# Layer two's attention for the even tokens on VectorE, beside layer one's second GEMM for the odd tokens

## The chip, the cores and the metric

The kernel runs on one core of one Trainium2 chip. The metric is the device time of one execution in microseconds (us); lower is better. A profiled execution gives the trace that the text reads. PE is TensorE, DVE is VectorE, ACT is ScalarE, SP is the engine whose queue issues every DMA of this kernel.

## The reference

Two layers of the same form, on 2048 tokens of width 1024, in bf16. Each layer first adds an attention of 32 heads of width 32, in which a token looks at itself and at the seven tokens 2, 4, ..., 14 places before it, and then adds a token-mixing MLP of hidden width 3584. Both read a layer norm without gains.

```python
W, dil = 8, 2
idx = pos[:, None] - (jnp.arange(W) * dil)[None, :]
logits = einsum("bhsd,bhswd->bhsw", q, kg) * scale     # kg, vg: k and v gathered at idx
logits = where(idx >= 0, logits, -1e9)
o = einsum("bhsw,bhswd->bhsd", softmax(logits), vg)    # then @ wo
u = gelu(einsum("bsd,sf->bdf", layernorm(x), w1) + b1)
y = einsum("bdf,fs->bds", u, w2) + b2
# x = x + attention(layernorm(x)); x = x + y(layernorm(x)); both twice, same weights
```

Since the step is 2, even tokens look at even tokens alone and odd ones at odd ones. The MLP mixes all tokens.

## The kernel before

Tokens are kept by class: `c` is 0 for even and 1 for odd tokens, `i` counts the eight tiles of 128 tokens in a class (`SC` = 1024 tokens). `hT` holds the normalised activations, features on partitions, the columns in class order. Each of the two layers runs four stages in this order, all bound together by PE's program order:

1. The V projection, 16 tiles of 128 tokens (`v_proj`, line 337; in the first layer `V_`, line 255).
2. Attention, in 16 units of one head group `g` (four heads) and one class `c`. A unit has two visits `b`. A visit computes `scores` (line 383), ACT's exponential (line 386), the band `mask` on DVE (line 398), `values` (lines 414 to 431), and two of the four `qk_chunk` (line 352) of the next unit. A chunk's queries go to `qB`, four copies for four heads: two on DVE (line 363), two by SP's DMAs (line 365).
3. The output projection `out_proj` (line 467) with the residual and the layer norm. The first four of its 16 tiles lie in the last two visits.
4. `gemm1` (line 510) with gelu, and `gemm2` (line 553): for each `i` the weights `w2` are loaded once, and both classes are computed. A `gemm2` step (c, i) is 56 matmuls of 128x512; DVE then adds bias and residual (line 556, twice), and in the first layer takes the statistics (lines 180 and 182), ACT makes the factor (lines 174 and 175), DVE normalises (line 188), and SP issues the store of `xb` and the transposing DMA to `hT` (line 562).

The order on an engine is set when the program is built: a scheduler places the instructions, `chain_` and `tc.issue_after` force an order among those that they name, and at run time every engine and every queue works in its order. Buffers come from pools with a fixed number: the PSUM tiles `m` (2), `s` (2) and `acc` (1), the weights' pool `wp` (9 tiles, tag `w`), `x2p` (6). A new tile waits until the tile whose place it takes is free. `qB`, `kT` and `Pm` have fixed places of their own before the change.

Of the kernel before, what the change touches and what calls it, by code (L numbers as in the profile page):

```python
# [17 lines left out]
W = 8  # L18
# [7 lines left out]
def kernel(  # L26
# [52 lines left out]
    pcp = pool("pcp", 2)  # L79
    dram = pool("dram", 1, space=bass.MemoryType.DRAM)  # L80
# [66 lines left out]

    hT = pers.tile([P, KD, S], BF16, name="hT")
    qB = [pers.tile([P, HG, SC + W], BF16, name=f"qB{n}") for n in range(2)]
    kT = [pers.tile([P, SC], BF16, name=f"kT{n}") for n in range(2)]  # L150
    Pm = pers.tile([P, HG, NS * HB, KW], BF16, name="Pm")

    def zero_fill():
        nc.vector.memset(Pm[:].rearrange("p h t k -> p (h t k)"), 0.0)
        for t in qB:
            r = nc.vector.memset(t[:].rearrange("p h t -> p (h t)"), 0.0)
        return r
# [8 lines left out]
    w1_v = B_w1.rearrange("(i p c) f -> c p i f", p=P, c=DIL)  # L166
    w2_v = B_w2.rearrange("(ft p) s -> p ft s", p=P)

    def rows(t, c, i):
        return t[(c * NI + i) * P:(c * NI + i + 1) * P, :]  # L170

# [156 lines left out]
    def fill_wv(wv, n):  # L328
        for hf in range(2):
            nc.sync.dma_start(out=wv[n][hf][:],  # L330
                              in_=wq_v[:, hf * (KD // 2):(hf + 1) * (KD // 2), 2 * D + n * 512:2 * D + (n + 1) * 512])

# [14 lines left out]
    def qk_chunk(u, wts, part, n):  # L347
        g, c = divmod(u, DIL)
# [44 lines left out]
    def mask(*rs):  # L393
        pc, s0 = exps
        for r in rs:
# [6 lines left out]
    def values(u, b, v, oT):  # L402
        g, c = divmod(u, DIL)
        acc = a_tile()
        t0 = b * HB
# [52 lines left out]
    def out_proj(c, i, oT, wo, res, dst, h2):  # L458
# [17 lines left out]
        def store():  # L476
            nc.sync.dma_start(out=rows(dst, c, i), in_=xn[:])
            h2[c][i] = vhp.tile([P, D], BF16, name="h2", tag="vh")
# [10 lines left out]
    def load_w1(fb):  # L489
        tiles = []  # L490
        for c in range(DIL):
            t = wt_("w1", [P, NI, FB])
            r = nc.sync.dma_start(out=t[:], in_=w1_v[c, :, :, fb * FB:(fb + 1) * FB])
# [6 lines left out]
    def gemm1(fb, h2, g):  # L500
        if fb not in w1s:
            load_w1(fb)
# [61 lines left out]
    NU = NG * DIL  # L564
    for li in range(2):
        first = li == 0
        v = [[None] * NI for _ in range(DIL)]
        for c, i in order:
            v[c][i] = vhp.tile([P, D], BF16, name="v", tag="vh")
# [6 lines left out]
        else:  # L576
            fill_wv(wv, 0)
            fill_wv(wv, 1)
            wts = [None, None]
            chain_("SP", load_qk, 0, wts)  # L580
            for i in range(NI):
                for c in range(DIL):
                    v_proj(v, c, i, wv, (0, 1))
            res = lambda c, i: rows(xb, c, i)
        oT = [gop.tile([P, S], BF16, name="oT", tag="go") for _ in range(NG)]
        h2 = [[None] * NI for _ in range(DIL)]
# [5 lines left out]
        for vis in range(2 * NU):  # L592
            u, b = divmod(vis, 2)
            if b == 0 and u % (2 * DIL) == 1 and u + 3 < NU:
                nxt = [None, None]
                chain_("SP", load_qk, u // (2 * DIL) + 1, nxt)
            if b == 0 and (u + 1) % (2 * DIL) == 0 and u + 1 < NU:
# [19 lines left out]
            for n in range(2):  # L617
# [3 lines left out]
                half, add, store, ln = out_proj(0, 2 * b + n, oT, wo, res, xa[li], h2)  # L621
# [12 lines left out]
        for k, (c, i) in enumerate(order[4:]):  # L634
            if k in (8, 10):
                chain_("SP", load_w1, k // 2 - 4)
            half, add, store, ln = out_proj(c, i, oT, wo, res, xa[li], h2)
# [10 lines left out]
        for fb in range(NFB):  # L648
            gemm1(fb, h2, g)
        if first:  # L650
            ln_exp_table()
        for i in range(NI):
            w2t = load_w2(i)
            w1s.clear()
            for c in range(DIL):
                gemm2(c, i, w2t, g, xa[li], rows(xb, c, i) if first else out_v[c, i], first)


# [28 lines left out]
```

The softmax here doesn't subtract the row's maximum and nothing guards it: scores larger than these inputs give would overflow.

## Time and profile before

| | us |
|---|---|
| median of three runs (lowest, highest) | 1298.24 (1298.19, 1298.45) |
| the profiled execution: its time / its span | 1297.71 / 1296.0 |
| PE busy / DVE busy / ACT busy | 1288.2 / 419.3 / 373.4 |
| first layer's `gemm2`, from its first matmul to the V projection after it | 457.84 to 651.06 |
| second layer's V projection, from its first matmul on | 651.06 to 706.48 |
| second layer's visits with `qk_chunk` (30 of 32) | 713.4 to 846.5 |

The span runs from the first to the last instruction that the profile shows; the time of the same execution is 1.7 us longer. The profiled execution is 0.5 us shorter than the median. Instructions of one engine are in order. A matmul's busy time overlaps that of the next one, since they are pipelined: what a matmul costs is read from the distance of the starts.

### The profile page before, as it was taken

To read this page: it belongs to the slowest core of one execution; us is meant where nothing else is said; L and a number is where in the kernel's file an instruction comes from. 1 tells how busy PE (TensorE), PEld (TensorE's weight loads), DVE (VectorE), ACT (ScalarE), POOL (GpSimd) and SP (SyncE) were. 2 spreads that over 40 slices of the span, in tenths; PEclk is the share of its full clock that TensorE was granted. 3 is DMA by queue.
4 is the path that set the end of the run, shared out by engine and by line. 5 is a ranking of instruction groups with operands and counts; after the bars stand their busy time and mean duration, and the time that the engine had idled before them with its cause. 6 is when DMAs were issued, how large, how long until landed. Compare 5 with 4: busy or idle time off the path is not lost.

```text
span 1296.0 us, 19495 instructions
## 1 busy us (share of the span) xinstructions
PE 1288.2 (99%) x8414; PEld 591.7 (46%) x8414; DVE 419.3 (32%) x851; ACT 373.4 (29%) x628; POOL 2.4 (0%) x15
## 2 busy tenths in 40 slices
PE   9999999999999999999999999999999999999998
PEld 4444444444444444444444444444444444444443
DVE  7457778810000022322300667688000000111111
ACT  5456665531111110000023666654211111000000
POOL 0000000000000000000000000000000000000000
PEclk9999999999999999999999999999999999999999
DMA  8411123652222235465510111246423222334330
GB/s 235 82 45 47 51 82 115 208 145 82 65 82 75 57 108 140 130 160 135 130 32 1 48 49 50 80 150 211 122 65 91 73 60 84 98 106 140 113 92 33
DMA packets 201574, 125.54 MB, mean 97 GB/s; under 512 B 39824, under 2 KB 183184, under 8 KB 201488
## 3 DMA queue, kind: packets, MB, share of 16 engines
q1 hardware_dynamic: 201488, 124.30, 33.8%
q8 instruction: 66, 1.08, 0.4%
q14 instruction: 20, 0.16, 0.0%
HBM read 96.48 MB, written 16.78 MB: 87 GB/s over the span
## 4 chain that ended last, share of the span: by engine, by line
PE 97%; DVE 1%; ACT 1%; issue 0%; DMA 0%; SPq 0%; DVEq 0%
PE m L352 17%; PE s L553 15%; PE s L510 15%; PE m L553 7%; PE m L510 7%; PE acc L510 7%; PE acc L553 7%; PE m L467 7%; PE m L337 4%; PE m L255 4%; PE s L383 2%; PE acc L418 1%; PE acc L422 1%; DVE xn L474 0%; PE m L268 0%; DVE Pm L398 0%
## 5 line engine op out<-in xcount | busy, mean ns | idle before, releaser
L510 PEld LDWEIGHTS <-w 128*128 128x128 bf16 x1792 | 175.4, 98 | 211.4
L553 PEld LDWEIGHTS <-w 128*128 128x128 bf16 x1792 | 175.3, 98 | 211.5
L352 PE MATMUL m<-hT,wqk 128*128 128x512 bf16 x1024 | 231.7, 380 | 0.0
L510 PE MATMUL s<-h,w 128*128 128x512 bf16 x896 | 202.8, 379 | 0.0
L553 PE MATMUL s<-g,w 128*128 128x512 bf16 x896 | 199.9, 379 | 0.0
L556 DVE SCALAR_TENSOR_TENSOR xo<-s,b_sb,xs 128x512 bf16<-128x512 f32 x32 | 24.0, 751 | 540.7 <-PE s L553 538.6
L352 PEld LDWEIGHTS <-wqk 128*128 128x128 bf16 x1024 | 95.3, 98 | 117.9 <-issue 10.7
L398 DVE TENSOR_TENSOR Pm<-pc,band 32x640 bf16<-32x640 bf16 x256 | 123.6, 483 | 65.8 <-ACT pc L386 56.3
L467 PE MATMUL m<-wo,oT 128*128 128x512 bf16 x512 | 112.5, 379 | 1.2 <-DVE xn L474 1.1
L510 PE MATMUL acc<-h,w 128*128 128x512 bf16 x448 | 103.9, 379 | 0.0
L553 PE MATMUL acc<-g,w 128*128 128x512 bf16 x448 | 100.6, 379 | 0.0
L553 PE MATMUL m<-g,w 128*128 128x512 bf16 x448 | 99.3, 379 | 0.0
L510 PE MATMUL m<-h,w 128*128 128x512 bf16 x448 | 99.0, 379 | 0.0
L174 ACT ACTIVATE ln<-mv,eps 128x1 f32<-128x1 f32 x64 | 18.9, 295 | 233.3 <-DVE mv L182 227.6
L517 ACT ACTIVATE g<-s,b_sb 128x1024 bf16<-128x1024 f32 x28 | 31.2, 1114 | 166.9 <-PE s L510 166.9
L467 PEld LDWEIGHTS <-oT 128*128 128x128 bf16 x512 | 49.5, 98 | 62.6 <-issue 4.5
L363 DVE COPY qB<-qs 32x512 bf16<-32x512 bf16 x136 | 38.1, 280 | 90.4 <-ACT qs L359 89.1
L255 PE MATMUL m<-wv,hT 128*128 128x512 bf16 x256 | 56.1, 379 | 0.7 <-ACT hT L249 0.7
L337 PE MATMUL m<-wv,hT 128*128 128x512 bf16 x256 | 55.4, 379 | 0.0
L359 ACT CAST qs<-m 128x512 bf16<-128x512 f32 x64 | 37.5, 586 | 49.0 <-PE m L352 49.0
L386 ACT ACTIVATE pc<-s,shift 128x640 bf16<-128x640 f32 x64 | 51.2, 799 | 0.3 <-PE s L383 0.3
L356 ACT CAST kT<-m 128x512 bf16<-128x512 f32 x64 | 37.5, 586 | 46.4 <-PE m L352 46.4
(57 smaller groups left out, 674.7 us busy)
## 6 DMA issues: line engine op xcount, KB each, us to landing
w<-in_B_w_dram SPq DMA_DIRECT2D x56, 512.0 KB, 3.8
w<-in_B_w_dram SPq DMA_DIRECT2D x64, 448.0 KB, 4.6
wqk<-in_A_wqkv_dram SPq DMA_DIRECT2D x16, 512.0 KB, 4.8
xa<-xn SPq DMA_DIRECT2D x32, 256.0 KB, 2.3
xs<-xa SPq DMA_DIRECT2D x32, 256.0 KB, 3.2
wv<-in_A_wqkv_dram SPq DMA_DIRECT2D x8, 512.0 KB, 5.5
wo<-in_A_wo_dram SPq DMA_DIRECT2D x8, 512.0 KB, 5.5
xr<-in_A_x_dram SPq DMA_DIRECT2D x16, 256.0 KB, 3.3
```

What stands on the lines that cost most here:

```text
L255: r = nc.tensor.matmul(pss_[k, n][:], lhsT=hT[:, kt, cols(*order[k])], rhs=wv[n][kt // 4][:, kt % 4, :], start=(kt == 0), stop=(kt == KD - 1))
L337: nc.tensor.matmul(ps[:], lhsT=hT[:, kt, cols(c, i)], rhs=wv[n][kt // 4][:, kt % 4, :], start=(kt == 0), stop=(kt == KD - 1))
L352: mm = nc.tensor.matmul(ps[:], lhsT=wts[part][:, kt, (g % 2) * P:(g % 2 + 1) * P], rhs=hT[:, kt, lo:lo + 512], start=(kt == 0), stop=(kt = ...
L356: nc.scalar.copy(out=kT[u % 2][:, ls], in_=ps[:])
L359: nc.scalar.copy(out=qs[:], in_=ps[:])
L363: nc.vector.tensor_copy(out=qB[u % 2][hp, h, ls], in_=qs[hp, :])
L386: nc.scalar.activation(out=pc[:].rearrange("p (n t) h k -> p n (t h k)", n=2), in_=ss[:, :, 0:2 * HG * GW], func=ACT.Exp, scale=scale, bia ...
L398: mm = nc.vector.tensor_tensor(out=Pm[rp, :, s0:s0 + HB, r * KG:r * KG + GW].rearrange("p h t k -> p t h k"), in0=pc[rp], in1=mk, op=ALU.mult)
L467: mm = nc.tensor.matmul(ps[:], lhsT=oT[g][:, cols(c, i)], rhs=wo[n][g // 4][:, g % 4, :], start=(g == 0), stop=(g == NG - 1))
L510: nc.tensor.matmul(pairs[fl][0][dc], lhsT=wt[c][:, i, fl * P:(fl + 1) * P], rhs=h2[c][i][:, dc * 512:(dc + 1) * 512], start=(k == 0), stop ...
L517: nc.scalar.activation(out=g[fb][:, fl, :].rearrange("p (n d) -> p n d", n=2), in_=t[:], func=ACT.Gelu_apprx_tanh, bias=b1_sb[:, ft:ft + 1])
L553: nc.tensor.matmul(aps[dc], lhsT=w2t[ft // HF][:, ft % HF, c::DIL], rhs=g[ft // GF][:, ft % GF, dc * 512:(dc + 1) * 512], start=(ft == 0), ...
```

## The change

In the second layer the attention of the even tokens leaves the units on PE, so that 16 units become 8 (the odd class alone). It is done by a class `Early`, which works while the first layer's `gemm2` still has odd tiles to do. The first layer's `gemm2` is reordered: all eight even tiles, the first odd tile, and then steps "C" (projections of one head group of the even tokens) alternate with the other odd tiles "G"; two C steps come first. The weights `w2` are now loaded once for each (c, i).

`Early` puts eight consecutive even tokens in each partition (token 8p + i in partition p, row i). `proj` computes q, k and v of one head group with `hT` columns of step 8 as the stationary operand: for each `i` eight matmuls with 256 moving columns and eight with 128. ACT copies q to `Q`, and k and v to rows 7 to 14 of `KV`, which has two places (`g % 2`). `halo` copies rows 8 to 14 of each partition to rows 0 to 6 of the next one, by one SBUF-to-SBUF DMA of 127 rows of 1792 elements. `qk` multiplies on DVE and adds in a tree, in two halves of four offsets each; `softmax` and `pv` follow one group later. The results go through eight transposing DMAs into `oT`, whose even columns are then in another order; `rows_p` and `w1_p` carry this order on. The tiles of `Early` share the places of `qB`, `kT` and `Pm`, which become pools.

```diff
+    atq = pool("atq", 2)
+    atk = pool("atk", 2)
+    atp = pool("atp", 1)
...
+    early = const.tile([P, W, NI], BF16, name="early")
+    nc.gpsimd.memset(early[:], 1.0)
+    nc.gpsimd.affine_select(out=early[:], in_=early[:], compare_op=ALU.is_ge, fill=0.0, base=1 - W,
+                            pattern=[[1, W], [1, NI]], channel_multiplier=NI)
...
+    def att_tiles():
+        qB[:] = [atq.tile([P, HG, SC + W], BF16, name="qB", tag="qB") for _ in range(2)]
+        kT[:] = [atk.tile([P, SC], BF16, name="kT", tag="kT") for _ in range(2)]
+        Pms[:] = [atp.tile([P, HG, NS * HB, KW], BF16, name="Pm", tag="Pm")]
 
...
+    w1_p = B_w1.rearrange("(p i c) f -> c p i f", i=NI, c=DIL)
+    def rows_p(t, c, i):
+        return t[c * SC:(c + 1) * SC, :].rearrange("(p i) d -> i p d", i=NI)[i]
 
...
+    def gemm2_first(c, i, w2t, k):
+        xs = x2("xs")
+        chain_("SP", lambda: nc.sync.dma_start(out=xs[:], in_=rows(xa[0], c, i)))
+        xo = x2("xo")
+        t = a_tile() if k % 3 == 2 else s_tile()
+
+        def mms():
+            for ft in range(FT):
+                for dc in range(NDC):
+                    r = nc.tensor.matmul(t[:, dc, :], lhsT=w2t[ft // HF][:, ft % HF, c::DIL],
+                                         rhs=g[ft // GF][:, ft % GF, dc * 512:(dc + 1) * 512],
+                                         start=(ft == 0), stop=(ft == FT - 1))
+            return r
+
+        def out():
+            for dc in range(NDC):
+                ds_ = slice(dc * 512, (dc + 1) * 512)
+                nc.vector.scalar_tensor_tensor(out=xo[:, ds_], in0=t[:, dc, :], scalar=b2_sb[:, i, c:c + 1],
+                                               in1=xs[:, ds_], op0=ALU.add, op1=ALU.add)
+            chain_("SP", lambda: nc.sync.dma_start(out=rows(xb, c, i), in_=xo[:]))
+            mean, rs = stats(xo, 1.0, eps1)
+            norm_dve(xs[:], xo[:], mean, rs)
+            chain_("SP", lambda: nc.sync.dma_start_transpose(out=hT[:, :, cols(c, i)], in_=xs[:]))
+
+        return mms, out
+
+    def load_w2c(i, tiles):
+        for n in range(NW2):
+            t = wt_("w2", [P, HF, 256])
+            r = nc.sync.dma_start(out=t[:], in_=w2_v[:, n * HF:(n + 1) * HF, i * 256:(i + 1) * 256])
+            tiles.append(t)
+        return r
+
+    TG = W // 2
+
+    class Early:
+        def __init__(self):
+            self.KV = atp.tile([P, 2, 2 * NI - 1, 2 * P], BF16, name="KV", tag="Pm")
+            nc.vector.memset(self.KV[0:1].rearrange("p b t k -> p (b t k)"), 0.0)
+            self.A = atq.tile([P, TG, NI, P], BF16, name="A", tag="qB")
+            self.Pe = atq.tile([P, TG, NI, P], BF16, name="Pe", tag="qB")
+            self.Q, self.wq, self.wv, self.S, self.EP, self.O = {}, {}, {}, {}, {}, {}
+
+        def load(self, g):
+            self.wq[g] = t = wt_("wqk", [P, KD, 2 * P])
+            for part in range(2):
+                r = nc.sync.dma_start(out=t[:, :, part * P:(part + 1) * P],
+                                      in_=wq_v[:, :, part * D + g * P:part * D + (g + 1) * P])
+            if g % 2 == 0:
+                self.wv[g] = self.wv[g + 1] = t = wt_("wv", [P, KD, 2 * P])
+                r = nc.sync.dma_start(out=t[:], in_=wq_v[:, :, 2 * D + g * P:2 * D + (g + 2) * P])
+            return r
+
+        def proj(self, g):
+            self.Q[g] = atk.tile([P, NI, P], BF16, name="Q", tag="kT")
+            for i in range(NI):
+                ps = m_tile()
+                for kt in range(KD):
+                    nc.tensor.matmul(ps[:, 0:2 * P], lhsT=hT[:, kt, i:SC:NI], rhs=self.wq[g][:, kt, :],
+                                     start=(kt == 0), stop=(kt == KD - 1))
+                for kt in range(KD):
+                    r = nc.tensor.matmul(ps[:, 2 * P:3 * P], lhsT=hT[:, kt, i:SC:NI],
+                                         rhs=self.wv[g][:, kt, (g % 2) * P:(g % 2 + 1) * P],
+                                         start=(kt == 0), stop=(kt == KD - 1))
+                nc.scalar.copy(out=self.Q[g][:, i, :], in_=ps[:, 0:P])
+                nc.scalar.copy(out=self.KV[:, g % 2, NI - 1 + i, :], in_=ps[:, P:3 * P])
+            return r
+
+        def halo(self, g):
+            return nc.sync.dma_start(out=self.KV[1:P, g % 2, 0:W - 1, :], in_=self.KV[0:P - 1, g % 2, NI:NI + W - 1, :])
+
+        def qk(self, g, hf):
+            A = self.A
+            if hf == 0:
+                self.S[g] = pcp.tile([P, W * NI * HG], FP32, name="S", tag="pc")
+            for j in range(TG):
+                s = hf * TG + j
+                nc.vector.tensor_tensor(out=A[:, j], in0=self.Q[g][:], in1=self.KV[:, g % 2, s:s + NI, 0:P], op=ALU.mult)
+            Av = A[:].rearrange("p j i (h d) -> p (j i h) d", d=DH)
+            n = TG * NI * HG
+            w = DH // 2
+            while w > 1:
+                nc.vector.tensor_tensor(out=Av[:, :, 0:w], in0=Av[:, :, 0:w], in1=Av[:, :, w:2 * w], op=ALU.add)
+                w //= 2
+            r = nc.vector.tensor_tensor(out=self.S[g][:, hf * n:(hf + 1) * n], in0=Av[:, :, 0], in1=Av[:, :, 1], op=ALU.add)
+            if hf:
+                self.EP[g] = pcp.tile([P, 2, W * NI * HG], BF16, name="EP", tag="pc")
+                nc.scalar.activation(out=self.EP[g][:, 0, :], in_=self.S[g][:], func=ACT.Exp, scale=scale, bias=shift[:])
+            return r
+
+        def softmax(self, g):
+            E, Pn = self.EP[g][:, 0, :], self.EP[g][:, 1, :]
+            Ev = E.rearrange("p (s h) -> p s h", h=HG)
+            mk = early[:].rearrange("p j i -> p (j i)").unsqueeze(2).to_broadcast([P, W * NI, HG])
+            nc.vector.tensor_tensor(out=Ev, in0=Ev, in1=mk, op=ALU.mult)
+            n = NI * HG
+            dn = x2("den", [P, 7 * n], FP32)
+            ds_ = [dn[:, 0:4 * n], dn[:, 4 * n:6 * n], dn[:, 6 * n:7 * n]]
+            nc.vector.tensor_tensor(out=ds_[0], in0=E[:, 0:4 * n], in1=E[:, 4 * n:8 * n], op=ALU.add)
+            nc.vector.tensor_tensor(out=ds_[1], in0=ds_[0][:, 0:2 * n], in1=ds_[0][:, 2 * n:4 * n], op=ALU.add)
+            nc.vector.tensor_tensor(out=ds_[2], in0=ds_[1][:, 0:n], in1=ds_[1][:, n:2 * n], op=ALU.add)
+            nc.vector.reciprocal(ds_[2], ds_[2])
+            return nc.vector.tensor_tensor(out=Pn.rearrange("p (j n) -> p j n", n=n), in0=E.rearrange("p (j n) -> p j n", n=n),
+                                           in1=ds_[2].unsqueeze(1).to_broadcast([P, W, n]), op=ALU.mult)
+
+        def pv(self, g, hf):
+            Pe = self.Pe
+            if hf == 0:
+                self.O[g] = vhp.tile([P, NI, P], BF16, name="o", tag="vh")
+            n = NI * HG
+            O = self.O[g]
+            for j in range(TG):
+                s = hf * TG + j
+                nc.scalar.copy(out=Pe[:, j].rearrange("p i (h d) -> p (i h) d", d=DH),
+                               in_=self.EP[g][:, 1, s * n:(s + 1) * n].unsqueeze(2).to_broadcast([P, n, DH]))
+                nc.vector.tensor_tensor(out=Pe[:, j], in0=Pe[:, j], in1=self.KV[:, g % 2, s:s + NI, P:2 * P], op=ALU.mult)
+            nc.vector.tensor_tensor(out=Pe[:, 0:2], in0=Pe[:, 0:2], in1=Pe[:, 2:4], op=ALU.add)
+            if hf == 0:
+                return nc.vector.tensor_tensor(out=O[:], in0=Pe[:, 0], in1=Pe[:, 1], op=ALU.add)
+            nc.vector.tensor_tensor(out=Pe[:, 0], in0=Pe[:, 0], in1=Pe[:, 1], op=ALU.add)
+            return nc.vector.tensor_tensor(out=O[:], in0=O[:], in1=Pe[:, 0], op=ALU.add)
+
+        def to_oT(self, g, oT):
+            return nc.sync.dma_start_transpose(out=oT[g][:, 0:SC].rearrange("p (i q) -> p i q", q=P),
+                                               in_=self.O[g][:].rearrange("p i d -> p (i d)"))
+
     for li in range(2):
         first = li == 0
+        units[:] = [(g, c) for g in range(NG) for c in range(DIL) if first or c]
+        NU = len(units)
+        UP = 2 * NU // NG
+        att_tiles()
         v = [[None] * NI for _ in range(DIL)]
         for c, i in order:
-            v[c][i] = vhp.tile([P, D], BF16, name="v", tag="vh")
+            if first or c:
+                v[c][i] = vhp.tile([P, D], BF16, name="v", tag="vh")
         wv = load_wv()
         if first:
             start_up(v, wv)
...
             chain_("SP", load_qk, 0, wts)
             res = lambda c, i: xin_v[c, i]
         else:
-            fill_wv(wv, 0)
-            fill_wv(wv, 1)
+            chain_("SP", fill_wv, wv, 0)
+            chain_("SP", fill_wv, wv, 1)
             wts = [None, None]
             chain_("SP", load_qk, 0, wts)
+            zero_fill()
             for i in range(NI):
-                for c in range(DIL):
-                    v_proj(v, c, i, wv, (0, 1))
-            res = lambda c, i: rows(xb, c, i)
+                v_proj(v, 1, i, wv, (0, 1))
+            res = lambda c, i: (rows if c else rows_p)(xb, c, i)
         oT = [gop.tile([P, S], BF16, name="oT", tag="go") for _ in range(NG)]
+        if not first:
+            for n in range(NG):
+                chain_("SP", ea.to_oT, n, oT)
+        dst = lambda c, i: (rows if c or first else rows_p)(xa[li], c, i)
+        w1_c = [w1_v[c] if first else (w1_v if c else w1_p)[c] for c in range(DIL)]
...
-            gemm1(fb, h2, g)
-        if first:
-            ln_exp_table()
-        for i in range(NI):
-            w2t = load_w2(i)
-            w1s.clear()
-            for c in range(DIL):
-                gemm2(c, i, w2t, g, xa[li], rows(xb, c, i) if first else out_v[c, i], first)
-
-
+            gemm1(fb, h2, g, w1_c)
+        w1s.clear()
+        if not first:
+            for i in range(NI):
+                w2t = load_w2(i)
+                for c in range(DIL):
+                    gemm2(c, i, w2t, g, xa[1], out_v[c, i], False)
+            continue
+        ln_exp_table()
+        ea = Early()
+        steps = [("G", 0, i) for i in range(NI)] + [("G", 1, 0), ("C", 0), ("C", 1)]
+        for i in range(1, NI):
+            steps.append(("G", 1, i))
+            if i + 1 < NI:
+                steps.append(("C", i + 1))
+        wts_ = {}
+
+        def prefetch(k):
+            if k < len(steps):
+                if steps[k][0] == "G":
+                    wts_[k] = []
+                    chain_("SP", load_w2c, steps[k][2], wts_[k])
+                else:
+                    chain_("SP", ea.load, steps[k][1])
+
+        prefetch(0)
+        nk = 0
+        for k, sp_ in enumerate(steps):
+            prefetch(k + 1)
+            if sp_[0] == "G":
+                mms, fin = gemm2_first(sp_[1], sp_[2], wts_[k], nk)
+                nk += 1
+                chain_("PE", mms)
+                fin()
+                continue
+            n = sp_[1]
+            chain_("PE", ea.proj, n)
+            chain_("SP", ea.halo, n)
+            if n:
+                chain_("DVE", ea.softmax, n - 1)
+            chain_("DVE", ea.qk, n, 0)
+            if n:
+                chain_("DVE", ea.pv, n - 1, 0)
+            chain_("DVE", ea.qk, n, 1)
+            if n:
+                chain_("DVE", ea.pv, n - 1, 1)
+        chain_("DVE", ea.softmax, NG - 1)
+        for hf in range(2):
+            chain_("DVE", ea.pv, NG - 1, hf)
```

The built order of one round on the engines, for group n in step C(n), is this. DVE: `softmax`(n-1), `qk`(n) first half, `pv`(n-1) first half, `qk`(n) second half, `pv`(n-1) second half, with the eight DVE instructions of one odd `gemm2` tile strewn in. ACT: the exponential of group n, the `KV` copies of the first two rows of group n+1, then its other `Q` and `KV` copies, with four of the eight broadcast copies to `Pe` of group n between them. SP: `halo`(n), the next projection weights, the next tile's `xs`, `xb` and `hT`, the next `w2`, `halo`(n+1). After the last group ACT has its eight `Pe` copies ahead of the second layer's V copies.

## The prediction

> **What bounds the kernel now.** I read the page's engine shares and chain first, then the busy time by stretches, then the groups of the stages concerned, then the DMA issues.
>
> ```profile
> PE 1288.2 (99%) x8414; PEld 591.7 (46%) x8414; DVE 419.3 (32%) x851; ACT 373.4 (29%) x628; POOL 2.4 (0%) x15
> PE 97%; DVE 1%; ACT 1%; issue 0%; DMA 0%; SPq 0%; DVEq 0%
> 550.00:600.00 50.00, 50.00 (x233) 22.69 (x232) 14.60 (x25) 1.99 (x8) 0.00 (x0) 1.00 0.55 140
> 750.00:800.00 50.00, 49.72 (x648) 24.02 (x647) 35.61 (x81) 33.56 (x57) 0.00 (x0) 1.00 0.22 59
> ```
>
> The first two lines are the page's shares and the chain: PE is the bound everywhere. The other two are stretches (length, then busy time of PE, PEld, DVE, ACT and POOL, the granted clock, DMA share, GB/s). In the first layer's `gemm2` DVE has 35 of 50 us free and ACT 48: that is the room the new attention gets. In the second layer's visits PE is as full.
>
> **PE: removed and added.** Thirty visits with chunks take 713.4 to 846.5, 4.44 us each. Sixteen of them go: 71.0 us. Half of the V projection goes: 55.4/2 = 27.7. Of a visit's 4.44 us, 16 x 0.216 = 3.46 are projections (32 matmuls of 512 columns take 6.91 in the chain), and these come back in `proj`. So the attention that leaves PE is worth 0.98 x 16 = 16 us only. The price of `proj` comes from this:
>
> ```profile
> 9.15 0.62 PE L244 MATMUL s<-ident,x 128*128 128x128 bf16 x8
> 9.61 1.89 PE L255 MATMUL m<-wv,hT 128*128 128x512 bf16 x8
> ```
>
> Eight matmuls of 128 columns, each with its own weight load, take 0.46, so 57 ns each; 256 columns lie between 57 and 216, about 110. One row i is 8 x 110 + 8 x 57 = 1.34 us, a C step 10.7, eight of them 85.6. Net on PE: 71.0 + 27.7 - 85.6 = 13 us less. That is all there is to win.
>
> **DVE per head group.** No row shows a bf16 product of 1024 columns; the nearest are these (group, busy us, mean ns):
>
> ```profile
> L398 DVE TENSOR_TENSOR Pm<-pc,band 32x640 bf16<-32x640 bf16 x256 | 123.6, 483 | 65.8 <-ACT pc L386 56.3
> L474 DVE TENSOR_TENSOR xn<-m,xr 128x512 bf16<-128x512 f32 x64 | 43.8, 685 | 7.4 <-PE m L467 6.1
> L192 DVE TENSOR_SCALAR bi<-mv,rs 128x1 f32<-128x1 f32 x32 | 6.6, 207 | 1.4 <-ACT rs L175 1.2
> ```
>
> From the 640-column row with the 207 ns of a one-column instruction as fixed part, 1024 columns cost 0.65 us and 2048 cost 1.09; in proportion 0.77 and 1.55. I take the middle, 0.71 and 1.30, and 0.03 between neighbours (the four masks of a visit take 2.03 for 4 x 0.483). The dear end is the 512-column row, where one column costs about 1 ns: 1.2 and 2.3. Then a half of `qk` is 4 products, additions over 2048, 1024, 512 and 256 columns and a last one: 2.84 + 1.30 + 0.71 + 0.41 + 0.30 + 0.27 + 0.27 = 6.1. `pv`'s first half is 2.84 + 1.30 + 0.71 + 0.18 = 5.0, the second 5.8, of which 3.0 up to its last product. `softmax` has six small ones: 1.9. The odd tile's own work is 2 x 0.75 + 2 x 0.69 + 0.21 + 0.55, with gaps 3.8. A round of DVE is 6.1 + 5.0 + 6.1 + 5.8 + 1.9 + 3.8 = 28.7 us, against PE's 10.7 + 12.1 (`gemm2`: 193.2/16 a tile) = 22.8. DVE becomes the bound by its work alone.
>
> **The round is also a ring.** `KV` has two places, so the ACT copies of group n+1 wait until DVE's last product of `pv`(n-1) has read its place. They hold the two `m` tiles, so PE stops after two of eight rows. From that product (time 0): DVE ends `pv` and does `softmax`(n) by 2.8 + 1.9 + 0.1 = 4.8; ACT, which has a `Pe` copy of group n in its order before the fourth row, then needs four such copies and five pairs of `Q` and `KV` copies. Line 359 (512 columns, 586 ns) and line 517 against 521 (1114 and 684 ns for 1024 and 512, so 0.84 ns a column) give 0.27 + 0.37 for a pair and 1.05 for a `Pe` copy: 4.8 + 4.2 + 5 x 0.65 = 12.3. Then comes the halo, H. Then DVE, which has idled since 4.8, does `qk` and `pv` up to the next such product with the odd tile's work: 6.1 + 5.0 + 6.1 + 3.0 + 3.8 = 24.0. So a round is 36.3 + H.
>
> **The halo.** It moves 127 x 3584 bytes, 0.455 MB. Rows near it (issue, KB, us to landing) and the stretch of the last store:
>
> ```profile
> w<-in_B_w_dram SPq DMA_DIRECT2D x64, 448.0 KB, 4.6
> xa<-xn SPq DMA_DIRECT2D x32, 256.0 KB, 2.3
> qB<-qs SPq DMA_DIRECT2D x120, 32.0 KB, 1.9
> 1290.00:1296.00 6.00, 2.20 (x11) 0.78 (x8) 0.75 (x1) 0.00 (x0) 0.00 (x0) 1.00 0.11 44
> ```
>
> Spread over 16 engines it would land in 2.3 to 4.6 us, say 3.5. But each large copy in the list has 128 rows and `qB<-qs` 32, all of which divide into 16 equal shares; 127 is prime and divides into none. If one engine carries all: the last store moved 44 GB/s at a share of 0.11 of 16 engines, 25 GB/s an engine, so 18.2 us, and with the 1.9 of a small copy H = 20.1. The page's mean over all traffic, 124.30 MB at 33.8% of 16 engines, is 17.7 GB/s: 25.7 + 1.9 = 27.6. I take 20.1, since the store's long rows are nearest in kind and no row shows an uneven cut. The Trainium skill, "DMA: Bandwidth & Descriptors", section "Why a DMA increments its semaphore by 16 and not by 1", says that such a copy uses the largest number up to 16 that divides its row count, and names 127 partitions as one engine; no run here shows it yet, and it speaks against this change.
>
> **Behind the waits.** While `halo` waits for the `KV` copies on SP, the next wqk, `xs`, `xb`, `hT` and `w2` are queued behind; PE needs none of them before the next ring opens, so nothing. `w2` is loaded twice as often: a tile's four loads can be issued about 4.2 us (the tile's DVE and ACT work) + 1.2 (`hT`'s issue) after the tile before ends, and the first lands 4.6 later, 10.4 of 12.1; if that cover fails, some us over eight tiles. `oT`'s transposes and the other row orders lie beside 8 units of attention, at nothing. The memsets (2.8 + 2 x 1.8) lie under the V projection.
>
> **The sum.** `gemm2` starts at 457.8; nine tiles of 12.08 end at 566.6, C(0) at 577.3, C(1) at 588.0. Copies 0.7, halo(0) lands at 598.1; halo(1) follows on the same engine at 616.3. `qk`(0) ends at 610.3, so the first round starts at 616.3 and reaches its last product at 640.3. Five rounds of 56.4 give 922.3; copies and halo(7) 954.7; a round with the rest of `pv`(6) 24.0 + 2.8, `softmax`(7) 1.9: 983.4. ACT then makes two sets of four `Pe` copies with 2.8 of DVE between: 994.6. The V copies are queued behind these on ACT, so PE, which has long filled two `m` tiles, does the other 27.7 - 3.5 now: 1018.8. From this point the kernel before needed 1296.0 - 706.5 = 589.5; less 71.0 it is 518.5. Span 1537.3, with 1.7 around it 1539.0, against 1297.7 of the profiled execution (0.5 under the median).
>
> **Rivals.**
> 1. The halo is spread, H = 3.5: the first round ends at 620.1, rounds are 39.8, and the same steps give 819.1, 834.9, 863.6, 874.8, 899.0 and 1419. For it: no row shows one engine alone. Against it: 127 rows.
> 2. DVE runs the products and trees at 1 ns a column: a round grows by about 13 us, and with H = 20.1 the time is near 1640, with H = 3.5 near 1520. Against it: the 640-column row.
> 3. The copies don't wait for the other place, and DVE's 28.7 sets the round: about 1419 - 6 x 11.1 = 1352. Against it: the built order has ACT's `KV` copy wait for DVE.
> 4. Faster: DVE and ring hide under PE's 22.8 a round and the 13 us are kept, 1285. For this a round must fall by 17 us even with H = 3.5, and the tail too: after C(7) 44 us pass (0.7 + 3.5 + 26.8 + 1.9 + 11.2) before ACT is free, of which the last tile and two V tiles cover 15.6. The sign turns where what is left of both is under 13 us. Half the assumed DVE time would not do it.
>
> **How the numbers follow.** One engine's halo at the assumed DVE rate 0.62; spread 0.19; dear DVE 0.09; no ring 0.05; faster 0.03; within 0.2% 0.02 (about what a measurement here can tell from no change). The likeliest alone spans 1500 to 1590 (H from 17 to 27). The range goes down to rival 1 and up to half of rival 2: 1400 to 1600.
>
> **What would show it.** Right: `halo` to landing near 20 us, eight times; DVE's first product of each `qk` waiting for that DMA; ACT's first `KV` copy waiting for DVE; PE idle some 33 us a round. The page's PEclk may dip there; here it is 1.00 in all stretches, while the 14 start-up matmuls took 589 ns for 379. Wrong: halo landing under 5 us (rival 1), a 1024-column product over 1.0 us (rival 2), no idle time of DVE (rival 3), V copies not behind `Pe` copies (a tail shorter by 28 us).

## The result, and the profile after

The changed kernel takes 1557.98 us (median of 4 runs, 1556.6 to 1559.44); the kernel before, run beside it, takes 1298.3 (4 runs, 1298.19 to 1298.45). The ratio is 1.2, with a 95% interval of 1.1979 to 1.2021: slower by 259.7 us. The forecast was 1539; the measured time is 19 us above it, inside the range and inside the likeliest case's own range of 1500 to 1590. The profiled execution took 1557.3 us, its span is 1555.6.

These are the page's engine shares, its chain by engine and by line, and its row of granted PE clock (tenths of full speed in 40 slices of 38.9 us), of the kernel after:

```profile
PE 1307.5 (84%) x8232; PEld 651.1 (42%) x8374; DVE 546.9 (35%) x1039; ACT 414.0 (27%) x732; POOL 2.7 (0%) x17
PE 68%; DMA 14%; DVE 12%; ACT 2%; issue 2%; SPq 2%; DVEq 0%; ACTq 0%
PE s L528 12%; PE m L368 10%; DMA KV<-KV 10%; PE acc L528 6%; PE s L571 6%; PE m L528 6%; PE m L485 5%; PE m L270 3%; PE m L571 3%; PE acc L571 3%; PE m L640 3%; PE s L591 3%; DVE A L664 2%; DVE Pe L697 2%; DVE A L659 2%
PEclk9999999999999999776777677599999999999999
```

PE carried 97% of the chain before; now it carries 68%. The halo copy alone (`KV<-KV`) has 10%: seven of the eight copies lie on the chain, 149.6 us in all, and DVE's products and trees have most of its 12%. PE is busy for 19 us longer than before where 13 less were predicted. The granted clock is low in ten slices, 622 to 1011, which are those of the rounds and their ends, and matmuls take longer there.

The stretches that answer to the two shown of before (columns as there): the first nine tiles of the first layer's `gemm2` with the first C step (and the end of `gemm1` before them), and one round.

```profile
457.68:604.00 146.32, 129.71 (x644) 63.41 (x653) 30.22 (x54) 10.69 (x35) 0.00 (x0) 0.97 0.59 150
757.12:810.17 53.05, 27.76 (x182) 19.42 (x184) 24.84 (x43) 12.57 (x27) 0.00 (x0) 0.73 0.29 79
```

The first stretch starts where `gemm2` started before. After the change PE reaches `gemm2` 4.8 us later, as the chain shows (457.84 before):

```profile
455.72 6.91 PE m L528 x32
462.62 3.02 PE s L591 x14
```

PE was full in `gemm2` before. Now it waits already in the first nine tiles: they are 108.7 us of work (9 x 12.08) and take 125.9, from 462.62 to 588.52. Then PE waits 3.3 us for the weights of the first C step, which takes 12.4 us for 10.7. In a round PE works 28 of 53 us at a granted clock of 0.73. DVE works 24.84 of the 53, so no engine bounds the round.

The chain of waits over one round of the kernel after (start, length, what; short pieces and PE's later rows left out):

```profile
757.12 2.51 DVE A L659 x4
...
775.00 2.42 DVE Pe L697 x4
...
777.44 0.38 ACT KV L647
...
777.86 1.86 PE m L640 x8
779.73 0.85 PE m L643 x8
...
782.83 0.88 PE m L640 x8
783.71 0.50 PE m L643 x8
...
788.93 21.15 DMA KV<-KV
```

This is the ring of the prediction, step by step: DVE from its first `qk` product to its last `pv` product takes 20.3 us (to 777.42), the copies and PE's six rows 11.5 (to 788.93), the halo 21.2 (to 810.17). Together that is 53.0, against 24.0 + 12.3 + 20.1 = 56.4.

### The profile page after: what moved, and what is told of

It reads as the page before. It is cut to its first block, busy times and chain, and to the rows that moved or that the text cites. A ratio compares the mean times of both kernels' runs of the same rounds, so it can differ in the third digit from the quotient of the medians.

```text
span 1555.6 us, 19608 instructions
## 1 busy us (share of the span) xinstructions
PE 1307.5 (84%) x8232; PEld 651.1 (42%) x8374; DVE 546.9 (35%) x1039; ACT 414.0 (27%) x732; POOL 2.7 (0%) x17
## 4 chain that ended last, share of the span: by engine, by line
PE 68%; DMA 14%; DVE 12%; ACT 2%; issue 2%; SPq 2%; DVEq 0%; ACTq 0%
PE s L528 12%; PE m L368 10%; DMA KV<-KV 10%; PE acc L528 6%; PE s L571 6%; PE m L528 6%; PE m L485 5%; PE m L270 3%; PE m L571 3%; PE acc L571 3%; PE m L640 3%; PE s L591 3%; DVE A L664 2%; DVE Pe L697 2%; DVE A L659 2%
## 5 line engine op out<-in xcount | busy, mean ns | idle before, releaser
L640 PE MATMUL m<-wqk,hT 128*128 128x256 bf16 x512 | 86.1, 324 | 158.2 <-ACT KV L647 83.9
L368 PE MATMUL m<-hT,wqk 128*128 128x512 bf16 x724 | 167.8, 380 | 4.5 <-issue 3.3
L591 PE MATMUL s<-g,w 128*128 128x512 bf16 x600 | 137.4, 387 | 20.3 <-DMA w<-in_B_w_dram 19.3
L591 PEld LDWEIGHTS <-w 128*128 128x128 bf16 x896 | 88.1, 99 | 134.1 <-DMA w<-in_B_w_dram 27.3
L640 PEld LDWEIGHTS <-hT 128*128 128x128 bf16 x512 | 65.0, 152 | 168.6 <-issue 161.1
L695 ACT COPY Pe<-EP 128x1024 bf16<-128x1024 bf16 x64 | 64.3, 1049 | 209.9 <-DVE Pe L698 191.2
L659 DVE TENSOR_TENSOR A<-Q,KV 128x1024 bf16<-128x1024 bf16 x64 | 39.9, 687 | 205.3 <-DMA KV<-KV 205.2
L415 DVE TENSOR_TENSOR Pm<-pc,band 32x640 bf16<-32x640 bf16 x192 | 92.7, 483 | 54.4 <-ACT pc L402 47.3
L574 DVE SCALAR_TENSOR_TENSOR xo<-s,b_sb,xs 128x512 bf16<-128x512 f32 x16 | 12.0, 751 | 280.6 <-PE s L571 276.4
L368 PEld LDWEIGHTS <-wqk 128*128 128x128 bf16 x768 | 71.4, 98 | 88.6 <-issue 7.8
L599 DVE SCALAR_TENSOR_TENSOR xo<-s,b_sb,xs 128x512 bf16<-128x512 f32 x22 | 15.9, 746 | 259.7 <-PE s L591 203.0
L571 PE MATMUL s<-g,w 128*128 128x512 bf16 x442 | 99.6, 380 | 0.4
L591 PE MATMUL acc<-g,w 128*128 128x512 bf16 x272 | 62.5, 387 | 5.3 <-DMA w<-in_B_w_dram 4.9
```

The costliest lines, as they stand in the source:

```text
L368: mm = nc.tensor.matmul(ps[:], lhsT=wts[part][:, kt, (g % 2) * P:(g % 2 + 1) * P], rhs=hT[:, kt, lo:lo + 512], start=(kt == 0), stop=(kt = ...
L415: mm = nc.vector.tensor_tensor(out=Pm[rp, :, s0:s0 + HB, r * KG:r * KG + GW].rearrange("p h t k -> p t h k"), in0=pc[rp], in1=mk, op=ALU.mult)
L571: nc.tensor.matmul(aps[dc], lhsT=w2t[ft // HF][:, ft % HF, c::DIL], rhs=g[ft // GF][:, ft % GF, dc * 512:(dc + 1) * 512], start=(ft == 0), ...
L591: r = nc.tensor.matmul(t[:, dc, :], lhsT=w2t[ft // HF][:, ft % HF, c::DIL], rhs=g[ft // GF][:, ft % GF, dc * 512:(dc + 1) * 512], start=(f ...
L640: nc.tensor.matmul(ps[:, 0:2 * P], lhsT=hT[:, kt, i:SC:NI], rhs=self.wq[g][:, kt, :], start=(kt == 0), stop=(kt == KD - 1))
L659: nc.vector.tensor_tensor(out=A[:, j], in0=self.Q[g][:], in1=self.KV[:, g % 2, s:s + NI, 0:P], op=ALU.mult)
```

## The experiments

All of them start from the kernel after, except one that starts from the kernel before. The times of before beside them are 1298.24 (7 runs; beside the cut into 112 and 15 rows, the three places of V, the early `xs` and all three together) and 1298.61 (13 runs; beside the others).

**Is it the one engine?** My theory: the halo's 127 rows go to a single DMA engine. The rival: some 20 us are the price of any such copy between partitions, or of its place behind other transfers. The first experiment cuts the same copy in two, 112 and 15 rows.

```diff
-            return nc.sync.dma_start(out=self.KV[1:P, g % 2, 0:W - 1, :], in_=self.KV[0:P - 1, ...])
+            for lo, hi in ((1, 113), (113, P)):
+                r = nc.sync.dma_start(out=self.KV[lo:hi, g % 2, 0:W - 1, :], in_=self.KV[lo - 1:hi - 1, ...])
+            return r
```

> The halo is cut into two DMAs of 112 and 15 rows, nothing else changes. Theory (127 rows go through one DMA engine, and each round waits for it): to landing falls from 21 us to 3 to 6, a round from 53.1 to about 36 to 38, the time to 1410 to 1440 us. Rival (copies inside SBUF are slow in themselves, or DVE's own work sets the round): the landing stays above 12 us or the round above 48, the time above 1520.

Measured: 1429.68 us (2 runs, 1427.67 to 1431.7), ratio 1.1013 (1.0991 to 1.1035). 128 us come back by cutting the rows differently. The larger of the two copies in the DMA issues of this kernel (KB each, us from issue to landing):

```profile
KV<-KV SPq DMA_DIRECT2D x8, 392.0 KB, 3.6
```

Rounds take 36.4 us, 16.8 less than 53.2, which is about what the halo is shorter by. There is a second effect, on the queue. SP's timeline of the kernel after, and then that of this experiment, at the same place (start, length of the issue):

```profile
604.84 0.75 SPq L651 DMA_DIRECT2D KV<-KV  x1
605.68 21.64 SPq L611 DMA_DIRECT2D w<-in_B_w_dram  x4
627.42 1.44 SPq L651 DMA_DIRECT2D KV<-KV  x1
```

```profile
605.46 1.54 SPq L652 DMA_DIRECT2D KV<-KV  x2
607.10 4.21 SPq L611 DMA_DIRECT2D w<-in_B_w_dram  x4
```

Behind the one-engine halo SP is held for 21.64 us while it issues the same four weight loads that take it 4.21 us behind the split one. So halo(1) could not even be issued before halo(0) was through.

That it is one engine can be read from the kernel after itself. SP's last issue behind the last halo ends at 957.36; what is under way some us later is the halo's (columns of the stretches above, the last two are the DMA share and GB/s):

```profile
962.00:965.00 3.00, 0.00 (x0) 0.00 (x0) 0.00 (x0) 0.00 (x0) 0.00 (x0) 0.70 0.07 26
965.00:968.00 3.00, 0.00 (x0) 0.00 (x0) 0.00 (x0) 0.00 (x0) 0.00 (x0) 0.50 0.07 26
```

A share of 0.07 is one of 16 engines (0.0625), and it moves 26 GB/s, where the prediction took 25. The Trainium skill, "DMA: Bandwidth & Descriptors", section "Why a DMA increments its semaphore by 16 and not by 1", gives the rule that the engine count is the largest number up to 16 that divides the row count; the two kernels agree with it at 127 (21.2 us) and 112 (3.6 us).

**Is it the number of engines, or only that 127 is odd?** The next experiment gives each of the eight groups another first row count, with the rest of the rows in a second, small DMA.

```diff
         def halo(self, g):
-            return nc.sync.dma_start(out=self.KV[1:P, g % 2, 0:W - 1, :], in_=self.KV[0:P - 1, ...])
+            cut = 1 + (126, 112, 125, 124, 122, 121, 119, 127)[g]
+            for lo, hi in ((1, cut), (cut, P)):
+                if lo < hi:
+                    r = nc.sync.dma_start(out=self.KV[lo:hi, g % 2, 0:W - 1, :], in_=self.KV[lo - 1:hi - 1, ...])
+            return r
```

> The halo's rows are cut differently for each head group: a first DMA of 126, 112, 125, 124, 122, 121, 119 and 127 rows for groups 0 to 7, and a second one for what is left of 127. Theory (a copy uses as many engines as the largest divisor of its row count up to 16: 14, 16, 5, 4, 2, 11, 7, 1): from the issue to the first product behind it about 3.5 us for 126, 112 and 121, 4 to 5 for 119, 5 to 7 for 125 and 124, 10 to 12 for 122, 21 for 127; the time 1440 to 1460. Rival (only the plain cut into halves, or the length, matters): all but the 127 rows alike, or 126 rows as slow as 127.

Measured: 1470.7 us (2 runs, 1469.59 to 1471.8), ratio 1.1325 (1.1302 to 1.1347), 10 us over the expected span. Three of the halo pieces on the chain of this kernel, those of 126, 122 and 127 rows (the group of 112 rows is not on it):

```profile
607.38 3.30 DMA KV<-KV
...
739.98 11.53 DMA KV<-KV
...
863.65 20.73 DMA KV<-KV
```

From the first halo issue to the first product behind it, so with the second issue in it:

| rows | largest divisor up to 16 | us |
|---|---|---|
| 112 (the experiment before, seven groups) | 16 | 3.8 to 5.4 |
| 126 | 14 | 4.5 |
| 121 | 11 | 6.7 |
| 119 | 7 | 8.5 |
| 125 | 5 | 8.6 |
| 124 | 4 | 10.2 |
| 122 | 2 | 12.4 |
| 127 | 1 | 20.8 |

The order is that of the divisors; 16 and 14, and 7 and 5, lie too close to be told apart. 126 rows and 127 rows differ by a factor of 4.6, so neither the length nor the cut into two decides. The sizes were a miss: all but the 127 rows took longer than I had expected, by 0.4 to 3.5 us beyond the upper ends, 13 us in sum, which covers the 10 us. A part of it doesn't shrink with k. As an estimate, 0.455 MB at 25.5 GB/s are 17.9 us, which leaves 2.9 of the 20.8; with these 2.9 added, time in proportion to 1/k would give 11.5 us for 2 engines and 4.2 for 14, near the table, but 7.3, 6.4, 5.3 and 4.4 for 4, 5, 7 and 11, which is 2 to 3 us too short. Why, these runs do not show: the rows from different groups also have different other transfers beside them.

**Is the rest of the ring the two places of `KV`?** Here V gets three places and K two, in the same buffer. The room is taken from the pool `x2p` (6 to 4), so what that pool does is changed too. K lies in place `g % 2`, V in `2 + g % 3`; the halo and the products (not shown) go by these places. K and V then need a halo each, both still of 127 rows.

```diff
-    x2p = pool("x2p", 6)
+    x2p = pool("x2p", 4)
...
-            self.KV = atp.tile([P, 2, 2 * NI - 1, 2 * P], BF16, name="KV", tag="Pm")
+            self.KV = atp.tile([P, 5, 2 * NI - 1, P], BF16, name="KV", tag="Pm")
...
-                nc.scalar.copy(out=self.KV[:, g % 2, NI - 1 + i, :], in_=ps[:, P:3 * P])
+                nc.scalar.copy(out=self.KV[:, g % 2, NI - 1 + i, :], in_=ps[:, P:2 * P])
+                nc.scalar.copy(out=self.KV[:, 2 + g % 3, NI - 1 + i, :], in_=ps[:, 2 * P:3 * P])
```

> V gets three places instead of two (K keeps two, the pool x2p falls from 6 to 4 buffers, the halo is two DMAs of 127 rows, one for K and one for V, half as large each). Theory (the copies of group n+1 wait for pv of group n-1, and copies and halo lie behind one another in a ring): copies and K's halo move under DVE's work, DVE's wait for the halo falls from 28 us a round to 5 to 15, a round to 32 to 42, the time to 1440 to 1500. Rival (the one-engine transfer alone sets the round): the round stays near 53, the time above 1530.

Measured: 1496.44 us (2 runs, 1495.81 to 1497.08), ratio 1.1527 (1.1504 to 1.155): 61.5 us less. A round falls from 53.2 us to 43.8, which is 2 us above the span expected for it; the time is inside its own. The waits (engine and line, releaser, us in all, times, longest), of the kernel after and then of this one:

```profile
DVE A L659 <- DMA KV<-KV: 205.2, 8, 28.4
...
PE m L640 <- ACT KV L647: 83.9, 8, 14.6
```

```profile
DVE A L663 <- DMA KV<-KV: 117.7, 8, 18.0
...
PEld L591 <- DMA w<-in_B_w_dram: 54.8, 13, 10.9
```

PE's wait for ACT's `KV` copies falls from 83.9 us to 3.5, and DVE's wait for the halo by 87.5: the copies no longer wait for DVE's last product. In place of these waits SP's queue comes forward: weight loading waits 54.8 us for `w2` (27.3 in the kernel after), as `w2` and `xs` stand behind slow issues. The smaller `x2p` has no run of its own.

**What cost the first nine tiles their cover?** In the kernel after, halo(0) is issued at 604.84; the prediction had 578.0. Of these 26.8 us, 4.8 lie before `gemm2`, 17.1 in the nine tiles, 3.3 in the wait for the first projection weights, and 1.7 in the first C step, whose first row is slow. `xs` stands behind the next tile's four `w2` loads on SP. The chain between two even tiles of the kernel after:

```profile
483.60 5.95 DMA xs<-xa
...
489.67 1.41 DVE xo L599 x2
...
493.69 1.24 SPq L604
...
495.02 4.14 DMA w<-in_B_w_dram
...
499.20 10.10 PE s L591 x46
```

PE waits for `w2` (499.20), `w2` for SP's transposing issue ahead of it (493.69), that for DVE, and DVE for `xs` (489.55), which was issued only after the next tile's `w2`. From the fourth on, two tiles take about 30.5 us instead of 24.2. The experiment issues `xs` of a tile one step earlier, ahead of the next `w2`.

```diff
         def prefetch(k):
             if k < len(steps):
                 if steps[k][0] == "G":
+                    xs_[k] = x2("xs")
+                    chain_("SP", lambda: nc.sync.dma_start(out=xs_[k][:], in_=rows(xa[0], *steps[k][1:])))
                     wts_[k] = []
                     chain_("SP", load_w2c, steps[k][2], wts_[k])
```

> The residual load xs of each gemm2 tile of the first layer is issued one step earlier, ahead of that step's w2 loads, nothing else changes. Theory (xs queued behind w2 delays DVE, the transposing DMA and so the next w2 in a ring): the first nine tiles take 109 to 113 us as in the kernel before, C(0) starts 20 to 28 us earlier, the time falls to 1528 to 1540. Rival (twice the w2 traffic is the limit itself): the nine tiles stay above 125 us, the time stays within 5 us of 1558.

Measured: 1537.97 us (4 runs, 1535.81 to 1538.54), ratio 1.1848 (1.1829 to 1.1868): 20 us less. The nine tiles take 108.8 us (461.70 to 570.48), which is their work alone, and the first C step follows at once. halo(0) is issued at 582.05, 22.8 us earlier and 4 behind the prediction, and the rounds stay at about 53.

The 4 us are older than `gemm2`: here too PE reaches it 3.9 us late. The chain of the kernel after points at one place, in the first layer's output projection, for which the prediction had no term. `Early`'s memset of row 0 of `KV`, on one partition, stands in DVE's order there (timelines of DVE and PE):

```profile
225.07 3.26 DVE L620 MEMSET KV<- 1x3840 uint32 x1 [0.73 <-issue]
229.52 10.80 PE L485 MATMUL m<-wo,oT 128*128 128x512 bf16 x41 [2.66 <-DVE xn L492]
```

An attention tile's normalisation and a residual of the output projection follow it on DVE, and PE waits for these; before the change PE runs through there. No run moves the memset, so its price is not shown.

The rival, that the double loading of `w2` costs bandwidth, is tried in the kernel before by its order of `gemm2` alone, all even tiles first, `w2` for each tile, nothing of `Early`:

```diff
-        for i in range(NI):
-            w2t = load_w2(i)
+        for c, i in (order if first else [(c, i) for i in range(NI) for c in range(DIL)]):
+            if first or c == 0:
+                w2t = load_w2(i)
             w1s.clear()
-            for c in range(DIL):
-                gemm2(c, i, w2t, g, xa[li], rows(xb, c, i) if first else out_v[c, i], first)
+            gemm2(c, i, w2t, g, xa[li], rows(xb, c, i) if first else out_v[c, i], first)
```

> The kernel before, with the first layer's gemm2 in the new order alone: all even tiles, then all odd ones, w2 loaded for each tile; attention as before. Here each xs is issued ahead of three of the next four w2 loads. Theory (not the doubled w2 traffic costs, but xs behind w2): gemm2 stays within 5 us of 193.2, the time within 0.4% of the kernel before. Rival (the doubled traffic costs about 3 us a tile): gemm2 takes 235 to 245 us, the time 1335 to 1350.

Measured: 1297.95 us (10 runs, 1297.43 to 1298.78), ratio 0.9996 (0.9987 to 1.0006). `gemm2` takes 193.4 us for 193.2. The doubled traffic and the new order cost nothing by themselves; the place of `xs` in SP's order does, as the run before showed.

**All three together.** The split halo, V's three places and the early `xs` (with `x2p` at 4):

> The three edits of halo_split, v_three and xs_early together. Theory (halo, ring and xs add up, DVE's work of 25 to 28 us a round is what is left): rounds of 27 to 31 us, the time 1330 to 1375, still slower than the kernel before. Rival (PE sets the round once the waits are gone): rounds of 23 us, the time below 1320.

Measured: 1385.23 us (2 runs, 1383.34 to 1387.12), ratio 1.067 (1.0649 to 1.0692), 10 us over the span expected. The three cuts are worth 128.3, 61.5 and 20.0 us alone, 209.8 in sum, and 172.8 together. Rounds take 32.0 us, not 27 to 31. The stretch of one round and, from the chain of waits, the ring that ends where it starts:

```profile
665.51:697.25 31.74, 25.51 (x185) 18.05 (x184) 24.97 (x44) 13.18 (x35) 0.00 (x0) 0.89 0.54 131
```

```profile
643.37 1.23 ACT Pe L697 x2
...
647.58 0.18 ACT KV L646
647.80 1.87 PE m L638 x8
...
660.66 4.73 DMA KV<-KV
665.51 2.51 DVE A L661 x4
```

DVE is busy 24.97 of 31.74 us, so it is not the bound even here. Another ring has opened: ACT makes its four `Pe` copies for `pv`'s second half (from 643.37) only when DVE has released the buffer, the `Q` and `KV` copies of the next group are queued behind them, PE's rows wait for these copies (the first row again slow, 1.87 us for its eight larger matmuls, where 0.88 is usual), and SP issues two pairs of halo DMAs behind a `w2` load. So this experiment does not measure DVE's floor. This ring is read from the chain; no run opens it.

**Would half of DVE's work do?** The kernel of all three, with the offsets 4 to 7 left out of the products of `qk` and `pv` (a copy stands for the second half of the logits; ACT's copies and products of the second half of `pv` are left out):

> all_three with the offsets 4 to 7 left out of qk and pv (the scores of offsets 0 to 3 stand in for them), so that the output is another; DVE's and ACT's work of a head group is about halved. Theory (DVE's work still lies in the ring with copies and halo): rounds fall from 32 to 23 to 26 us, the time to 1310 to 1345, still slower than the kernel before. Rival (with half the work the new attention is hidden under PE): rounds 22.8 and the time below 1298.

Measured: 1343.11 us (2 runs, 1341.46 to 1344.76), ratio 1.0342 (1.0322 to 1.0363). The time is in the expected span; the rounds, 26.5 to 28.1 us, are above the 23 to 26 expected. In the round of 28.14 DVE is busy 14.89 and PE 23.59:

```profile
681.79:709.93 28.14, 23.59 (x178) 16.41 (x176) 14.89 (x28) 8.86 (x31) 0.00 (x0) 0.94 0.52 130
```

With 40% of DVE's round gone, the kernel is still 3.4% slower than before. What is left on the chain of that round is the ring through ACT, PE's first row, SP and a halo of 4.7 us; its parts, and the ends of the stage, have no run of their own.

**Is the tail worth moving?** The kernel of all three, with the last group's `softmax` and `pv` written behind the second layer's V projection:

```diff
-            zero_fill()
             for i in range(NI):
                 v_proj(v, 1, i, wv, (0, 1))
+            chain_("DVE", ea.softmax, NG - 1)
+            for hf in range(2):
+                chain_("DVE", ea.pv, NG - 1, hf)
+            att_tiles()
+            zero_fill()
...
-        chain_("DVE", ea.softmax, NG - 1)
-        for hf in range(2):
-            chain_("DVE", ea.pv, NG - 1, hf)
```

> all_three with the last group's softmax and pv written behind the second layer's V projection, so that ACT can copy V tiles before the last broadcast copies. Theory (PE waits at the end for ACT, whose V copies are queued behind the last group): 8 to 18 us less than all_three, 1367 to 1377. Rival (the tail is set by DVE's last products, which the odd units wait for): within 5 us of 1385.

Measured: 1380.79 us (4 runs, 1377.37 to 1383.88), ratio 1.0631 (1.0607 to 1.0655). That is 4.4 us less than all three, within the rival's 5 us and not clear of noise: the runs and the two intervals overlap. The gain that my theory put on the V copies behind `Pe` copies is not there. The chain at the end of the V projection:

```profile
847.82 0.59 ACT v L355
...
851.05 1.22 DVE Pe L700
...
857.45 1.78 DVE qB L167
...
861.61 0.29 PE s L399
```

Most V copies now run ahead of or between these copies and PE doesn't stop in the V projection (818.92 to 847.79), but the first `scores` of the second layer (861.61) need `qB`, whose place is that of `Pe`; so the last `pv` and the memsets are the end anyway: these first `scores` start at 861.61, and at 864.09 without the move. The wait has moved, not gone.

## Why the prediction held, point by point

The prediction's marks against the trace (us from the span's start; the last column is what each stretch between marks adds to the error):

| mark | predicted | measured | added |
|---|---|---|---|
| halo(0) issued | 578.0 | 604.84 | +26.8 |
| first product of `qk`(0) | 598.1 | 626.7 | +1.8 |
| first round starts | 616.3 | 650.76 | +5.9 |
| `qk`(7) starts | 954.7 | 969.81 | -19.4 |
| last `Pe` copies | 994.6 | 1006.93 | -2.8 |
| V projection ends | 1018.8 | 1033.35 | +2.2 |
| the rest | 518.5 | 522.2 | +3.7 |

**What bounds, and the ring.** Right. The halo on one engine, DVE's first product waiting for it eight times (205.2 us), ACT's `KV` copy waiting for DVE's last product, PE idle through much of each round (25 us, not 33, as its work takes 28 us at the low clock): all are there as written, at 53.2 us a round (319.05 over the six from 650.76 to 969.81) for 56.4.

**The halo, H.** Right: 20.1 predicted from the 25 GB/s of one engine in the last store, 21.2 measured, at 26 GB/s and a DMA share of one engine. The scan shows the reason, the divisor of the row count, in eight sizes. What was missed beside it is the queue: "PE needs none of them before the next ring opens, so nothing" holds in the rounds for another reason: PE does wait there for the next wqk (74.3 us in eight waits), but its first two rows are done at 764.6, 13 us before DVE's last product opens the ring at 777.42. And halo(1) is one of the issues behind. It was to follow 18.2 us after halo(0) and came 24.1 after (626.7 to 650.76), since SP was held until 627.42.

**The first nine tiles.** This is the term that was mis-sized. The prediction took "10.4 of 12.1" as covered and "some us over eight tiles" if not; up to the first halo it was some 22 of the 26.8 us. The sum had DVE start right after the tile's matmuls, and left out that its input `xs` is queued behind the next tile's `w2`. Waiting 5.95 us for it in the chain, DVE is late, then the transposing DMA, then the next `w2`. Issuing `xs` earlier took 22.8 us off and left the nine tiles at their work. The other 4.8 us, the later start of `gemm2`, had no term at all.

**DVE per round.** Too dear: 28.7 predicted, 24.84 busy. (The odd tile has six instructions on DVE in a round, as the sum had it, not the eight of the built order given with the change.) The groups by form of the kernel after (busy, mean ns):

```profile
L659 DVE TENSOR_TENSOR A<-Q,KV 128x1024 bf16<-128x1024 bf16 x64 | 39.9, 687 | 205.3 <-DMA KV<-KV 205.2
L698 DVE TENSOR_TENSOR Pe<-Pe 128x2048 bf16<-128x2048 bf16 x16 | 19.6, 1222 | 0.3
```

One product takes 0.687 us for 0.71 and the 2048 columns 1.222 for 1.30, each close. But the sum added 0.03 between neighbours, where four independent products start every 0.60 to 0.63 us (2.41 to 2.51 for four) and the odd tile's instructions fit between the dependent additions of the trees. From the first product to the last of a round this made 20.3 for 24.0, which is most of the -19.4 of the table over six rounds. That this offset most of the +26.8 was luck: the total is nearer than its parts.

**The copies and projections between.** 11.5 for 12.3, so right in size, but the carrier was often another. The prediction ran the chain over ACT (`Pe` copies, then five pairs of copies); in four of the six rounds the trace runs it over PE's six rows, 10.5 us, and in the other two (from 704.21 and 863.90) over `softmax` and a `Pe` copy, as predicted, and then over PE's last three rows. A row costs 1.37 us against 1.34 predicted once PE is at speed, but the first two after the idle time take 2.71 and 2.25, 4.96 in sum. The granted clock is 0.50 in the windows from 769.00 to 782.29 and 1.00 from there to 788.34: PE is idle for 13.3 us before these rows, begins them at 777.86 at the low clock, and has the full clock 4.4 us later. The Trainium skill, "TensorE: Matmul & The Clock Gate", Part 1, says that the clock falls to half after an idle window of about 3.4 us and returns after a busy one. These rows agree with it.

**The tail.** Right in size (26.4 us from the last `Pe` copies to the end of the V projection, 24.2 predicted), and the V copies do stand behind the `Pe` copies, but moving them lowered the median by only 4.4 us, within the noise: `qB` and `Pe` share their places, so DVE's end sets the next stage.

**The rivals.** The first (halo spread) was 1419; with the halo spread the chip gave 1429.7, with the same two errors of opposite sign in it (rounds of 36.4 us for 39.8). The second (1 ns a column) is out: 1222 ns for 2048 columns. The third (no ring, DVE sets the round, 1352) was not reached by three cuts at once, 1385, as another ring took over. The fourth (faster) said that half the assumed DVE time would not do it: at half the offsets, with the halo spread and the other two edits in, the kernel is still 3.4% slower than before.

**What is not settled.** Why copies on 4 to 11 engines take 2 to 3 us longer than in proportion; how much of the 4.8 us before `gemm2` is the memset; and how much of the waits for `w` and `xs` with three V places is due to the smaller `x2p` pool that pays for them.

## What to carry to other kernels

Look at the row count of every partition copy before its bytes: 127 rows here went through one DMA engine at 21 us, and cutting them as 112 + 15 took about 4 and gave 128 us back. When work is moved to a free engine, write out the ring of buffer reuse (who frees which place, who waits for it) before adding up busy times: here no engine bounded the round, and with three edits together another ring took over. And price a prefetch by everything that stands in front of it in its queue, including the small input that was put behind it.

## What the runs showed of the hardware that I had not expected

- A 127-row copy alone in flight kept one of 16 DMA engines busy (a share of 0.07) at 26 GB/s.
- A copy on one DMA engine holds the queue of the engine that issues it: four weight loads behind it kept SP for 21.64 us, against 4.21 behind a split one.
- From issue to the first product behind it, time falls more slowly than 1/k: 20.8, 12.4, 10.2, 8.6, 8.5, 6.7 and 4.5 us for row counts with the divisors 1, 2, 4, 5, 7, 11 and 14, and 3.8 to 5.4 for 16.
- Independent DVE products of 128x1024 bf16 start every 0.60 us although each is recorded with 0.687; dependent additions of 2048 columns, recorded with 1.22, start 1.26 before the next.
- Loading `w2` twice over 193 us of `gemm2` changed the time by a factor of 0.9996 (0.9987 to 1.0006).
